# Long convolution and gate on one core: in the last phase VectorE joins at the end of each quarter, transposes follow two rows later, the first x rows load first, and constant matmuls stand between the phases

## The chip, the cores and the metric

One core of a Trainium2 chip runs the whole kernel. The metric is the device time of one execution in microseconds; lower is better. All data is float32.

## The reference

Two steps, one after the other: a long convolution of `u = x * v` with a filter made from `pos_emb`, gated by x, and then a short gate over the result.

```python
h_filt = (np.maximum(pos_emb @ w1, 0.0) @ w2) * np.exp(-0.01 * pos)[:, None]
u = x * v                                     # (4, 12800, 128)
y = irfft(rfft(u, 2 * S) * rfft(h_filt, 2 * S))[:, :S]
x = x * y                                     # goes into the second step
gate_pre = sum(conv_w[k] * x_shifted_by(4 - k) for k in range(5))
out = (sigmoid(gate_pre) * (x @ w_val)) @ w_out
```

## The kernel before, in words

The sequence of 12800 is cut into J = 2 halves of N1 x N2 = 100 x 64, and the transforms are done as matmuls with tables of cosines and sines. There are three phases.

**Phase one** (to about 420 us) transforms along N1, prepares the filter, and writes `a_u` to memory.

**Phase two** (420 to 848 us) goes over 50 pairs of frequencies: it loads `a_u` and a table, multiplies with the filter's spectrum, transforms back along N2, and writes `c_y` to memory (line 378, from ScalarE's queue). The last pair's matmuls are `c_ps` (line 368), its copy `c_sb` (line 375).

**Phase three** (from 848 us) is what the change is about. Its order of instructions is written out by hand (`tc.manual_schedule()`), in the loop at line 573. It works on 32 groups of R = 4 rows. A step `t` of the loop holds three groups at once: group `s = t + 3` gets its rows of y, group `t` its taps, group `t - 1` its value, gate product and projection. One pass of the inner loop over `r` is called a quarter here; a quarter handles one row of each of the three groups:

- `y_sum` (PE, line 492): the last inverse transform of a row, out of two tiles of `c_y`, into `sd` in PSUM. `y_copy` (ScalarE, line 499) copies it to `sd_sb`.
- `y_trans`: four transposes (PE, line 506) into `tp3`, and the copy of one half of it to `dif` (ScalarE, line 508).
- `y_join`: sum and difference of the halves (VectorE, lines 516 and 517) into `yr`, and the product with the x row (GpSimd, line 519) into `ext`.
- `tap` (VectorE, line 534): one term of the short convolution for a whole group, accumulated in `gt`; a group has taps 1 to 4, one in each quarter. Tap 0 is ScalarE's (line 531), and so is the `sigmoid` behind tap 4 (line 538).
- `value` (PE, line 543), `gated` (the gate product, VectorE, line 548), `project` (PE, line 553), `finish` (ScalarE's copy of the output row, line 561, and after four rows the output's DMA, line 564).
- Once in four groups `fill_halo` copies rows between `ext` tiles on ScalarE.

The loads of a group come from SP's queue (`load_rows`): two tiles of `c_y`, each split by rows 96 and 4, and one tile of x rows (line 459). All loads of the kernel share one pool, `ld`, of six buffers; a new tile takes the buffer that came free first. A `c_y` buffer is free after the group's last `y_sum`, an x buffer after the group's last product. SP issues in order, and so does each engine.

Of the kernel before, what the change touches and what calls it, by code (L numbers as in the profile page):

```python
# [9 lines left out]
F32 = mybir.dt.float32  # L10
# [13 lines left out]
B, S, D, FO, KC = 4, 12800, 128, 64, 5  # L24
# [2 lines left out]
KG = 8  # L27
P1C = 2
R = 4
NC1 = N1 // 2 + 1  # L30


def _tables():
# [5 lines left out]
    inv = np.zeros((N1, 2, N2))  # L39
    inv[:, 0, :NC1] = (np.cos(th.T) + np.sin(th.T))[:, :NC1] / (2 * M)  # L40
    inv[:, 1, :NC1] = (np.cos(th.T) - np.sin(th.T))[:, :NC1] / (2 * M)
    ph = (np.outer(4 * k1 + 1, n2)[:, :, None] + 4 * N1 * np.outer(n2, k2)[None]) % (4 * M)
# [62 lines left out]
def tile_longconv_gate(  # L105
# [20 lines left out]
    nc = tc.nc  # L126
# [13 lines left out]
    dft = const.tile([128, 2, 2 * N2], F32, name="dft")  # L140
    tw = const.tile([128, 2, N1], F32, name="tw")
    ident = const.tile([128, 128], F32, name="ident")
# [19 lines left out]
    def load():  # L162
        return ld.tile([128, 2048], F32, name="ld")
# [276 lines left out]
    with tc.tile_pool(name="p3", bufs=1) as p3, tc.tile_pool(name="ps3", bufs=1, space=PSUM) as ps3:  # L440
        HALO = KC - 1
        ROW = B * N1
        NG = N2 // R
        EG = 4
        assert HALO == R
        groups = [(j, g) for j in range(J) for g in range(NG)]
        y_order = [(j, g) for j in range(J) for g in [NG - 1] + list(range(NG - 1))]
        tails, exts, loads3, sds, tps, gate_sg, gate_gt, outs3 = {}, {}, {}, {}, {}, {}, {}, {}

        def load_rows(s):  # L450
            j, g = y_order[s]
            ct = []
            for c in range(2):
                t = load()[:N1]
                n0 = c * N2 + g * R
                sync_s.dma_start(out=t, in_=c_y[j].rearrange("k p b d -> k p (b d)")[:, n0:n0 + R].rearrange("k p e -> k (p e)"))
                ct.append(t)
            xr = load()[:, 0:R * ROW]
            nc.sync.dma_start(out=xr, in_=xt[j][:, g * R:(g + 1) * R].rearrange("d n b a -> d (n b a)"))
            loads3[s] = ct, xr  # L460

        def place(j, g):

            if g == NG - 1 and (j, g // EG) not in exts:
                return tails[j], 0
            return exts[j, g // EG], HALO + g % EG * R

        def new_ext(j, q):
            e = p3.tile([D, HALO + EG * R, B, N1], F32, name="ext", bufs=2)
            exts[j, q] = e  # L470
# [17 lines left out]
        def y_sum(s, r):  # L488
            ct, _ = loads3[s]
            sd = ps3.tile([128, B * D], F32, name="sd", bufs=2)  # L490
            for c in range(2):
                nc.tensor.matmul(  # L492
                    out=sd[c * N2:(c + 1) * N2], lhsT=inv[:, c], rhs=ct[c][:, r * B * D:(r + 1) * B * D],
                    start=True, stop=True)
            sds[s, r] = sd

        def y_copy(s, r):
            t = p3.tile([128, B, D], F32, name="sd_sb", bufs=3)
            nc.scalar.copy(out=t.rearrange("p b d -> p (b d)"), in_=sds.pop((s, r)))  # L499
            sds[s, r] = t  # L500

        def y_trans(s, r):
            t = sds.pop((s, r))
            tp = ps3.tile([D, B, 128], F32, name="tp3", bufs=2)
            for b in range(B):
                nc.tensor.transpose(out=tp[:, b], in_=t[:, b], identity=ident)  # L506
            dif = p3.tile([D, B, NC1], F32, name="dif", bufs=3)
            nc.scalar.copy(out=dif, in_=tp[:, :, N2:N2 + NC1])
            tps[s, r] = tp, dif

        def y_join(s, r):
            tp, dif = tps.pop((s, r))
            j, g = y_order[s]
            xr = loads3[s][1].rearrange("d (n b a) -> d n b a", n=R, b=B)[:, r]
            yr = p3.tile([D, B, N1], F32, name="yr", bufs=3)
            nc.vector.tensor_tensor(yr[:, :, 0:NC1], tp[:, :, 0:NC1], dif, op=ALU.add)  # L516
            nc.vector.tensor_tensor(yr[:, :, NC1:N1], tp[:, :, 1:NC1 - 1], dif[:, :, 1:NC1 - 1], op=ALU.subtract)  # L517
            e, r0 = place(j, g)
            nc.gpsimd.tensor_tensor(e[:, r0 + r], yr, xr, op=ALU.mult)  # L519

        def rows(t, k=HALO):
            j, g = groups[t]
            e = exts[j, g // EG].rearrange("d n b a -> d (n b a)")
            r0 = g % EG * R + k
            return e[:, r0 * ROW:(r0 + R) * ROW]

        def tap(t, k):
            if k == 0:
                gt = p3.tile([D, R * ROW], F32, name="gt", bufs=2)
                gate_gt[t] = gt  # L530
                nc.scalar.activation(gt, rows(t, 0), AF.Copy, scale=cw[:, 0:1])  # L531
            else:
                gt = gate_gt[t]
                nc.vector.scalar_tensor_tensor(gt, rows(t, k), cw[:, k:k + 1], gt, op0=ALU.mult, op1=ALU.add)  # L534

        def sigmoid(t):
            sg = p3.tile([D, R * ROW], F32, name="sg", bufs=2)
            nc.scalar.activation(sg, gate_gt.pop(t), AF.Sigmoid)  # L538
            gate_sg[t] = sg

        def value(t, r):
            v_ps = ps3.tile([D, ROW], F32, name="v_ps", bufs=2)
            nc.tensor.matmul(out=v_ps, lhsT=wval, rhs=rows(t)[:, r * ROW:(r + 1) * ROW], start=True, stop=True)  # L543
            return v_ps

        def gated(t, r, v_ps):
            gd = p3.tile([D, ROW], F32, name="gd", bufs=3)
            nc.vector.tensor_tensor(gd, v_ps, gate_sg[t][:, r * ROW:(r + 1) * ROW], op=ALU.mult)  # L548
            return gd

        def project(gd):
            o_ps = ps3.tile([D, ROW], F32, name="o_ps", bufs=2)
            nc.tensor.matmul(out=o_ps, lhsT=wout, rhs=gd, start=True, stop=True)  # L553
            return o_ps

        def finish(t, r, o_ps):
            if r == 0:
                o_sb = p3.tile([D, R * ROW], F32, name="o_sb", bufs=2)
                outs3[t] = o_sb
            o_sb = outs3[t]  # L560
            nc.scalar.copy(out=o_sb[:, r * ROW:(r + 1) * ROW], in_=o_ps)
            if r == R - 1:
                j, g = groups[t]
                nc.scalar.dma_start(
                    out=out[j][:, g * R:(g + 1) * R].rearrange("d n b a -> d (n b a)"), in_=outs3.pop(t))

        AHEAD3, NT = 3, len(groups)
        y_last = gd_last = o_last = None  # L570
        with tc.manual_schedule():
            load_rows(0)
            for t in range(-AHEAD3, NT + 2):
                s = t + AHEAD3
                if s + 1 < NT:
                    load_rows(s + 1)
                if 0 <= s < NT:
                    j, g = y_order[s]
                    if g == NG - 1:
                        tails[j] = p3.tile([D, R, B, N1], F32, name="tail", bufs=2)  # L580
                    elif g % EG == 0:
                        new_ext(j, g // EG)
                for r in range(R):
                    if y_last is not None:
                        y_trans(*y_last)
                    v_ps = value(t - 1, r) if 0 <= t - 1 < NT else None
                    if s < NT:
                        y_sum(s, r)
                    if o_last is not None:
                        finish(*o_last)  # L590
                        o_last = None
                    if gd_last is not None:
                        o_last = gd_last[0], gd_last[1], project(gd_last[2])
                        gd_last = None
                    if 0 <= t < NT:
                        tap(t, r + 1)
                    if r == R - 1 and 0 <= t < NT:
                        sigmoid(t)
                    if y_last is not None:
                        y_join(*y_last)  # L600
                        y_last = None
                    if v_ps is not None:
                        gd_last = t - 1, r, gated(t - 1, r, v_ps)
                    if s < NT:
                        y_copy(s, r)
                        y_last = s, r
                    if r == 1 and s < NT and g % EG == 0:
                        fill_halo(j, g // EG)
                    if r == 2 and 0 <= t + 1 < NT:
                        tap(t + 1, 0)  # L610


_INS = ["x", "v", "pos_emb", "w1", "w2", "moe_w_val", "moe_conv_w", "moe_w_out"]
# [34 lines left out]
```

## Time and profile before

| | us |
|---|---|
| three runs | 1342.48, 1333.96, 1340.4 (median 1340.4) |
| the profiled execution | 1342.08 |
| its span | 1340.2 |
| mean granted clock of TensorE | 0.938 |

The page gives busy time for each engine. PE is TensorE's matmuls, PEld its weight loads, DVE VectorE, ACT ScalarE, POOL GpSimd, SP the engine that issues loads; a "q" behind an engine is its queue. A row of a timeline has the start in us, the length in us, the engine, the line of the kernel, the operation, output and inputs by the program's names; "[... <- ...]" is the idle time of the engine before it, and what ended it. A granted clock of 0.50 is TensorE at half speed. A float32 matmul stands in the trace as two records.

### The profile page before, as it was taken

The numbers are of one execution on the slowest core, as the hardware profiler recorded it, in microseconds if no ns is written. First come the engines' busy times: TensorE is split into PE (matmuls) and PEld (weight loads), VectorE is DVE, ScalarE is ACT, GpSimd is POOL, SyncE is SP. The second block draws the span as 40 slices with busy tenths as digits, with TensorE's granted clock in tenths as the row PEclk, the third lists the DMA queues.
The fourth block names the chain that finished last, engine by engine and source line by source line (L and its number), as shares of the span: only waits on it lengthen the run. The fifth ranks groups of instructions, "written<-read, shape, count | busy, mean of one in ns | idle before, by whom it ended". The sixth has DMA issues, their size and how long they took to land. (4 is left out here: it accounts for less than half of the span.)

```text
span 1340.2 us, 16163 instructions
## 1 busy us (share of the span) xinstructions
PE 1184.8 (88%) x5464; PEld 554.0 (41%) x5464; DVE 1068.8 (80%) x1130; ACT 635.5 (47%) x1064; POOL 693.8 (52%) x346
## 2 busy tenths in 40 slices
PE   4879999788686899999999999578999898999986
PEld 3657877566452333333333333122333333333332
DVE  5875343988456999999999999127999999999997
ACT  3334545677442333333333333134665666666663
POOL 2333234444454799999999999234333333333230
PEclk8888899889888999999999999656999999999999
DMA  9999788889987677778787874766989898889842
GB/s 250 285 312 297 232 253 271 245 268 306 296 261 285 219 278 280 281 277 279 280 280 279 280 266 173 209 160 157 254 236 246 234 243 243 244 247 243 241 145 98
DMA packets 144571, 332.90 MB, mean 248 GB/s; under 512 B 11166, under 2 KB 63434, under 8 KB 136554
## 3 DMA queue, kind: packets, MB, share of 16 engines
q1 hardware_dynamic: 96576, 226.13, 57.9%
q10 hardware_dynamic: 47914, 105.76, 21.7%
q8 instruction: 43, 0.70, 0.2%
q14 instruction: 38, 0.31, 0.1%
HBM read 200.77 MB, written 131.07 MB: 248 GB/s over the span
## 5 line engine op out<-in xcount | busy, mean ns | idle before, releaser
L534 DVE SCALAR_TENSOR_TENSOR gt<-ext,cw,gt 128x1600 f32<-128x1600 f32 x128 | 298.3, 2330 | 0.0
L258 POOL TENSOR_TENSOR u_lo<-u_t,u_hi 100x1024 fp32r<-100x1024 f32 x64 | 158.7, 2483 | 239.0 <-ACT u_hi L257 199.9
L519 POOL TENSOR_TENSOR ext<-yr,ld 128x400 f32<-128x400 f32 x120 | 134.1, 1117 | 280.4 <-DVE yr L517 275.1
L375 ACT COPY c_sb<-c_ps 128x1024 f32<-128x1024 f32 x100 | 101.3, 1013 | 275.3 <-PE c_ps L368 275.3
L340 PE MATMUL z_ps<-ld 128*64 128x512 f32 x800 | 194.4, 605 | 7.8 <-DMA ld<-a_u 6.6
L427 POOL TENSOR_TENSOR va<-va,vb 128x1024 f32<-128x1024 f32 x50 | 158.0, 3160 | 37.1 <-DVE vb L345 37.0
L281 PE MATMUL fp<-u_hi,fwd_hi 100*100 100x512 f32 x256 | 117.8, 460 | 55.2 <-ACT st L284 26.4
L492 PE MATMUL sd<-ld,inv 100*64 100x512 f32 x512 | 155.6, 681 | 9.8 <-issue 7.7
L286 DVE COPY st<-fp 100x512 f32<-100x512 f32 x128 | 85.4, 685 | 71.8 <-PE fp L281 52.9
L345 DVE TENSOR_TENSOR vb<-z_ps,h_sb 128x2048 f32<-128x2048 f32 x50 | 114.5, 2291 | 24.9 <-ACT c_sb L375 24.7
L506 PE MATMUL tp<-ident,sd_sb 128*128 128x128 f32 x512 | 90.7, 304 | 45.7 <-ACT sd_sb L499 45.7
L499 ACT COPY sd_sb<-sd 128x512 f32<-128x512 f32 x128 | 74.6, 583 | 115.5 <-PE sd L492 115.4
L553 PE MATMUL o_ps<-gd,wout 128*128 128x400 f32 x256 | 119.4, 548 | 8.4 <-DVE gd L548 8.2
L428 POOL TENSOR_TENSOR vc<-vc,vd 128x1024 f32<-128x1024 f32 x50 | 118.5, 2370 | 15.2 <-DVE vd L345 10.3
L256 DVE TENSOR_TENSOR u_t<-ld 100x1024 f32<-100x1024 f32 x64 | 86.9, 1359 | 48.4 <-POOL u_lo L258 33.6
L345 DVE TENSOR_TENSOR va<-z_ps,h_sb 128x2048 f32<-128x2048 f32 x50 | 114.0, 2281 | 11.0 <-DMA ld<-a_u 11.0
L429 POOL TENSOR_TENSOR va<-va,vb 128x1024 f32<-128x1024 f32 x50 | 118.6, 2371 | 0.0
L506 PEld LDWEIGHTS tp<-ident,sd_sb 128*128 128x128 f32 x512 | 58.6, 151 | 132.9 <-ACT sd_sb L499 132.9
L281 PE MATMUL fp<-u_hi,fwd_lo 100*100 100x512 f32 x256 | 110.0, 430 | 0.0
L368 PE MATMUL c_ps<-vc,ld 64*128 64x512 f32 x400 | 100.6, 621 | 10.7 <-DVE vc L418 10.6
L543 PE MATMUL v_ps<-ext,wval 128*128 128x400 f32 x256 | 108.5, 506 | 0.0
L257 ACT CAST u_hi<-u_t 100x1024 fp32r<-100x1024 f32 x64 | 68.0, 1064 | 77.4 <-PE fp L281 37.0
(76 smaller groups left out, 1895.6 us busy)
## 6 DMA issues: line engine op xcount, KB each, us to landing
c_y<-c_sb ACTq DMA_DIRECT2D x100, 512.0 KB
ld<-a_u SPq DMA_DIRECT2D x49, 1024.0 KB
ld<-c_y SPq DMA_DIRECT2D x64, 768.0 KB
ld<-in_xt_dram SPq DMA_DIRECT2D x32, 800.0 KB
out_dram<-o_sb ACTq DMA_DIRECT2D x32, 800.0 KB
ld<-in_x_dram SPq DMA_DIRECT2D x64, 384.0 KB
ld<-in_v_dram SPq DMA_DIRECT2D x64, 384.0 KB
a_u<-st ACTq DMA_DIRECT2D x64, 384.0 KB
```

Of the source, the lines that this page charges most:

```text
L258: nc.gpsimd.tensor_tensor(lo, u_t, hi.bitcast(F32), op=ALU.subtract)
L281: nc.tensor.matmul(out=fp, lhsT=w[:, c], rhs=d[:, b:b + 2], start=(k == 0), stop=(k == 2))
L340: nc.tensor.matmul(out=z[half[h]], lhsT=wk[:, h, half[c]], rhs=a2[:, h, j], start=True, stop=True)
L345: nc.vector.tensor_tensor(out, z.rearrange("p (b d) -> p b d", d=D).unsqueeze(1).to_broadcast([128, n, B, D]), h_sb.unsqueeze(2).to_broadc ...
L427: nc.gpsimd.tensor_tensor(va[:, 0:2], va[:, 0:2], vb[:, 0:2], op=ALU.add)
L428: nc.gpsimd.tensor_tensor(vc, vc, vd, op=ALU.add)
L429: nc.gpsimd.tensor_tensor(va[:, 2:4], va[:, 2:4], vb[:, 2:4], op=ALU.add)
L492: nc.tensor.matmul(out=sd[c * N2:(c + 1) * N2], lhsT=inv[:, c], rhs=ct[c][:, r * B * D:(r + 1) * B * D], start=True, stop=True)
L506: nc.tensor.transpose(out=tp[:, b], in_=t[:, b], identity=ident)
L519: nc.gpsimd.tensor_tensor(e[:, r0 + r], yr, xr, op=ALU.mult)
L534: nc.vector.scalar_tensor_tensor(gt, rows(t, k), cw[:, k:k + 1], gt, op0=ALU.mult, op1=ALU.add)
L553: nc.tensor.matmul(out=o_ps, lhsT=wout, rhs=gd, start=True, stop=True)
```

## The change

The row of y that a quarter transposes and joins is now the row summed two quarters earlier (`LAG = 2`, kept in the list `y_run`); it was the row of the quarter before. The joins move behind the gate product. Tap 0 of the next group moves from the third quarter to the fourth, and the sigmoid behind the copy of the sums. The x rows of the first three groups are loaded ahead of all `c_y` tiles. Forty matmuls of two constant tables stand ahead of the first sum; nothing reads their result.

```diff
+WARM = 40
...
+        def load_x(s):
+            j, g = y_order[s]
+            xr = load()[:, 0:R * ROW]
+            nc.sync.dma_start(out=xr, in_=xt[j][:, g * R:(g + 1) * R].rearrange("d n b a -> d (n b a)"))
+            loads3[s] = xr
...
-            xr = load()[:, 0:R * ROW]
-            nc.sync.dma_start(out=xr, in_=xt[j][:, g * R:(g + 1) * R].rearrange("d n b a -> d (n b a)"))
-            loads3[s] = ct, xr
+            if s not in loads3:
+                load_x(s)
+            loads3[s] = ct, loads3[s]
...
-        AHEAD3, NT = 3, len(groups)
-        y_last = gd_last = o_last = None
+        AHEAD3, NT, LAG = 3, len(groups), 2
+        y_run, gd_last, o_last = [], None, None
         with tc.manual_schedule():
+            for s in range(AHEAD3):
+                load_x(s)
             load_rows(0)
+
+            for _ in range(WARM):
+                w_ps = ps3.tile([D, 2 * D], F32, name="o_ps", bufs=2)
+                nc.tensor.matmul(
+                    out=w_ps, lhsT=ident, rhs=dft.rearrange("p a k -> p (a k)"), start=True, stop=True)
...
                 for r in range(R):
-                    if y_last is not None:
-                        y_trans(*y_last)
+                    done = y_run.pop(0) if len(y_run) == LAG or s >= NT and y_run else None
+                    if done:
+                        y_trans(*done)
...
                     if 0 <= t < NT:
                         tap(t, r + 1)
+                    if r == R - 1 and 0 <= t + 1 < NT:
+                        tap(t + 1, 0)
+                    if v_ps is not None:
+                        gd_last = t - 1, r, gated(t - 1, r, v_ps)
+                    if done:
+                        y_join(*done)
+                    if s < NT:
+                        y_copy(s, r)
+                        y_run.append((s, r))
                     if r == R - 1 and 0 <= t < NT:
                         sigmoid(t)
-                    if y_last is not None:
-                        y_join(*y_last)
-                        y_last = None
-                    if v_ps is not None:
-                        gd_last = t - 1, r, gated(t - 1, r, v_ps)
-                    if s < NT:
-                        y_copy(s, r)
-                        y_last = s, r
                     if r == 1 and s < NT and g % EG == 0:
                         fill_halo(j, g // EG)
-                    if r == 2 and 0 <= t + 1 < NT:
-                        tap(t + 1, 0)
```

VectorE's instructions over two quarters in the middle of the phase, before (`yr` are the joins, `gd` the gate product, `gt` the tap; the numbers tell tiles apart):

```order
L516 TENSOR_TENSOR yr_6741<-tp3_6724,dif_6729 128x4x51
L517 TENSOR_TENSOR yr_6741<-tp3_6724,dif_6729 128x4x49
L548 TENSOR_TENSOR gd_6745<-v_ps_6731,sg_6682 128x400
L534 SCALAR_TENSOR_TENSOR gt_6664<-ext_6478,cw_75,gt_6664 128x1600
L516 TENSOR_TENSOR yr_6766<-tp3_6749,dif_6754 128x4x51
L517 TENSOR_TENSOR yr_6766<-tp3_6749,dif_6754 128x4x49
L548 TENSOR_TENSOR gd_6770<-v_ps_6756,sg_6682 128x400
L534 SCALAR_TENSOR_TENSOR gt_6664<-ext_6478,cw_75,gt_6664 128x1600
```

The same place in the change:

```order
L541 SCALAR_TENSOR_TENSOR gt_6749<-ext_6547,cw_75,gt_6749 128x1600
L555 TENSOR_TENSOR gd_6810<-v_ps_6800,sg_6759 128x400
L523 TENSOR_TENSOR yr_6812<-tp3_6793,dif_6798 128x4x51
L524 TENSOR_TENSOR yr_6812<-tp3_6793,dif_6798 128x4x49
L541 SCALAR_TENSOR_TENSOR gt_6749<-ext_6547,cw_75,gt_6749 128x1600
L555 TENSOR_TENSOR gd_6835<-v_ps_6825,sg_6759 128x400
L523 TENSOR_TENSOR yr_6837<-tp3_6818,dif_6823 128x4x51
L524 TENSOR_TENSOR yr_6837<-tp3_6818,dif_6823 128x4x49
```

Before, the gate product stands between the joins and the tap; now the tap follows the joins at once. (Lines of the change stand 7 further down.)

SP's queue from the last load of phase two on, before:

```order
L358 DMA ld_5905<-a_u_63 128x2x1024
L101 DMA ld_6064<-c_y_64 96x2048
L101 DMA ld_6064<-c_y_64 4x2048
L101 DMA ld_6067<-c_y_64 96x2048
L101 DMA ld_6067<-c_y_64 4x2048
L459 DMA ld_6070<-in_xt_dram 128x1600
L101 DMA ld_6072<-c_y_64 96x2048
L101 DMA ld_6072<-c_y_64 4x2048
L101 DMA ld_6075<-c_y_64 96x2048
L101 DMA ld_6075<-c_y_64 4x2048
L459 DMA ld_6078<-in_xt_dram 128x1600
```

And in the change (`c_y` at line 102, x rows at line 454):

```order
L359 DMA ld_5905<-a_u_63 128x2x1024
L454 DMA ld_6064<-in_xt_dram 128x1600
L454 DMA ld_6066<-in_xt_dram 128x1600
L454 DMA ld_6068<-in_xt_dram 128x1600
L102 DMA ld_6070<-c_y_64 96x2048
L102 DMA ld_6070<-c_y_64 4x2048
L102 DMA ld_6073<-c_y_64 96x2048
L102 DMA ld_6073<-c_y_64 4x2048
L102 DMA ld_6156<-c_y_64 96x2048
L102 DMA ld_6156<-c_y_64 4x2048
L102 DMA ld_6159<-c_y_64 96x2048
```

Three x tiles stand first, so the sixth and last free buffer of the pool goes to the first `c_y` tile of the second group (`ld_6156`); the second one (`ld_6159`) needs a buffer to come free.

PE at the hand-over, before (`tp` are the transposes):

```order
L368 MATMUL c_ps<-vc,ld 128x512 x4
L492 MATMUL sd<-ld,inv 64x512 x2
L506 MATMUL tp_6086<-ident,sd_sb 128x128 x4
L492 MATMUL sd<-ld,inv 64x512 x2
L506 MATMUL tp_6102<-ident,sd_sb 128x128 x4
L492 MATMUL sd<-ld,inv 64x512 x2
```

And in the change:

```order
L369 MATMUL c_ps<-vc,ld 128x512 x4
L585 MATMUL o_ps<-dft,ident 128x256 x40
L499 MATMUL sd<-ld,inv 64x512 x4
L513 MATMUL tp_6173<-ident,sd_sb 128x128 x4
L499 MATMUL sd<-ld,inv 64x512 x2
L513 MATMUL tp_6189<-ident,sd_sb 128x128 x4
```

The forty constant matmuls come ahead of the first sums, and two rows are summed before the first is transposed.

## Prediction

> **What bounds the kernel now.** The page comes first, then the busy time by stretches, then the groups of the last phase, then its order of time. The profiled execution took 1342.1 us (span 1340.2 and 1.9 around it), 1.7 above the median of the three times; all sums below start from it. The last phase runs from about 848 us to the end.
>
> ```profile
> PE 1184.8 (88%) x5464; PEld 554.0 (41%) x5464; DVE 1068.8 (80%) x1130; ACT 635.5 (47%) x1064; POOL 693.8 (52%) x346
> ...
> 860.00:880.00 20.00, 15.74 (x41) 5.05 (x40) 3.23 (x11) 5.15 (x12) 5.14 (x5) 0.50 0.81 194
> ...
> 1100.00:1200.00 100.00, 92.43 (x362) 35.53 (x360) 99.59 (x120) 62.06 (x109) 32.75 (x30) 1.00 0.88 243
> ```
>
> Line one ranks PE first over the whole span. The stretches (after the length: busy us of PE, PEld, DVE, ACT, POOL, then granted clock, DMA share, GB/s) say otherwise for this phase: from 1100 to 1200 DVE is busy 99.59 of 100 us, so VectorE sets the pace; at 860 it has 3.23 of 20 us, and PE works at clock 0.50. So two stages must be costed apart: the steady stage, and the ramp before it.
>
> ```profile
> 1104.34 0.64 PE L506 MATMUL tp<-ident,sd_sb 128*128 128x128 f32 x4
> ...
> 1106.52 0.36 DVE L516 TENSOR_TENSOR yr<-tp,dif 128x204 f32<-128x204 f32 x1
> ...
> 1106.80 0.34 DVE L517 TENSOR_TENSOR yr<-tp,dif 128x196 f32<-128x196 f32 x1
> 1107.06 0.56 DVE L548 TENSOR_TENSOR gd<-v_ps,sg 128x400 f32<-128x400 f32 x1
> ...
> 1107.22 1.04 POOL L519 TENSOR_TENSOR ext<-yr,ld 128x400 f32<-128x400 f32 x1 [2.31 <-DVE yr L517]
> ...
> 1107.36 0.64 PE L506 MATMUL tp<-ident,sd_sb 128*128 128x128 f32 x4
> 1107.55 2.40 DVE L534 SCALAR_TENSOR_TENSOR gt<-ext,cw,gt 128x1600 f32<-128x1600 f32 x1
> ...
> 1107.84 0.84 PE L543 MATMUL v_ps<-ext,wval 128*128 128x400 f32 x2
> ...
> 1108.60 1.08 PE L492 MATMUL sd<-ld,inv 100*64 100x512 f32 x4
> ...
> 1109.61 0.94 PE L553 MATMUL o_ps<-gd,wout 128*128 128x400 f32 x2
> ...
> 1109.87 0.36 DVE L516 TENSOR_TENSOR yr<-tp,dif 128x204 f32<-128x204 f32 x1
> ```
>
> One quarter on VectorE is 1109.87 - 1106.52 = 3.35 us, without a gap: two joins (0.28 + 0.26), the gate product (0.49), the tap (2.32 to the next join). The join releases GpSimd's product, which starts 0.16 us after the gate product begins and is still running when the tap begins.
>
> ```profile
> 901.00 0.35 DVE L517 TENSOR_TENSOR yr<-tp,dif 128x196 f32<-128x196 f32 x1
> 901.27 1.88 DVE L534 SCALAR_TENSOR_TENSOR gt<-ext,cw,gt 128x1600 f32<-128x1600 f32 x1
> 901.43 2.63 POOL L519 TENSOR_TENSOR ext<-yr,ld 128x400 f32<-128x400 f32 x1 [2.90 <-DVE yr L517]
> ...
> 1306.11 1.87 DVE L534 SCALAR_TENSOR_TENSOR gt<-ext,cw,gt 128x1600 f32<-128x1600 f32 x1
> 1307.90 0.56 DVE L548 TENSOR_TENSOR gd<-v_ps,sg 128x400 f32<-128x400 f32 x1
> ```
>
> In the first group of taps there is no gate product yet, so the tap follows the join at once: 1.88 us, and GpSimd's product takes 2.63. After the last product the tap alone takes 1.87. So a tap costs 0.52 more when the product starts before it, and nothing when it starts first; then the product pays 1.6.
>
> **The change, part by part.** *Join last.* The quarter becomes tap, gate product, two joins, tap: the order of 901.00 to 901.27 in every quarter. VectorE then needs 1.79 (1306.11 to 1307.90) + 0.49 + 0.28 + 0.27 = 2.83 us, 11.3 a group of four. The product would end 2.8 us after the tap's start (0.16 + 2.63), before the next tap.
>
> What is late next is PE. From 1104.34 to 1107.36 it goes round in 3.02: transposes 0.48, value 0.76, sums 1.01, projection 0.77. That is 12.1 a group. Today it also waits for the copied rows.
>
> ```profile
> L506 PE MATMUL tp<-ident,sd_sb 128*128 128x128 f32 x388 | 62.7, 284 | 28.9 <-ACT sd_sb L499 28.9
> ...
> 1028.40:1030.40 2.00, 0.99 (x7) 0.58 (x6) 2.00 (x2) 1.36 (x2) 1.00 (x1) 1.00 0.78 188
> 1030.40:1036.40 6.00, 6.00 (x25) 2.24 (x24) 6.00 (x9) 2.62 (x6) 2.08 (x2) 1.00 1.02 234
> 1036.40:1041.00 4.60, 4.60 (x20) 1.62 (x18) 4.60 (x5) 3.39 (x6) 1.04 (x1) 1.00 0.93 320
> 1041.00:1041.80 0.80, 0.80 (x4) 0.30 (x2) 0.80 (x4) 0.70 (x2) 0.05 (x1) 1.00 0.12 48
> ...
> 1096.33 1.45 SPq L101 DMA_DIRECT2D ld<-c_y  x4
> ...
> 1101.44 0.35 SPq L459 DMA_DIRECT2D ld<-in_xt_dram  x1
> ```
>
> *Transposes two rows behind.* The wait of 28.9 us (of the 330 between 960 and 1290) is for the copy of the row before; a row more between copy and transpose (3 us) covers it, also where ScalarE puts tap 0 and the sigmoid in between. No work is added. Left alone, PE would go at its 12.1.
>
> ```profile
> 1107.19 1.63 ACT L531 ACTIVATE gt<-ext,cw 128x1600 f32<-128x1600 f32 x1
> ...
> 1109.98 1.54 ACT L538 ACTIVATE sg<-gt 128x1600 f32<-128x1600 f32 x1 [0.55 <-DVE gt L534]
> ```
>
> *Tap 0 and sigmoid later.* Both now stand in the last quarter, the sigmoid behind the copy of the sums: 3.2 us of ScalarE at one place, a little more than a quarter. Once a group VectorE's next gate product waits for the sigmoid, by my reading some 0.8 us, which is just its slack against PE (12.1 - 11.3): cost 0. Without that slack it is 27 x 0.8 = 22 us.
>
> The third bound is DMA. A group's transfers fill 12.6 of 13.4 us (1028.40 to 1041.00), c_y for some 8.0 us, then x rows and output; as a share 0.88 x 13.4 = 11.8 us if packed without gaps. Issue moves as well: SP's x load waits for the product that frees its buffer. It came 5.1 us behind the c_y loads (1096.33, 1101.44) and will come one quarter (3.0) and 1.6 of longer product later, at 9.7. SP's queue holds the next c_y loads behind it, but those wait until 12.1 anyway. So the new wait sits in cover of 2.4 us; without it c_y would land late at the next group's first sum.
>
> Bounds for the group: 11.3 (VectorE alone) to 13.4 (DMA no better than now). I take the middle of PE's 12.1 and DMA's 12.6, 12.35, since both are close.
>
> ```profile
> 934.71 2.40 DVE L534 SCALAR_TENSOR_TENSOR gt<-ext,cw,gt 128x1600 f32<-128x1600 f32 x1
> ...
> 1299.96 2.39 DVE L534 SCALAR_TENSOR_TENSOR gt<-ext,cw,gt 128x1600 f32<-128x1600 f32 x1
> ```
>
> These are the first taps of groups 2 and 29: 365.25 us for 27 groups, 13.53 each with the groups that also copy the halo. **Steady stage: 27 x (13.53 - 12.35) = 31.9 us less.**
>
> *The gap.* Now the hand-over between the phases, and the loads.
>
> ```profile
> 844.30 2.65 PE L368 MATMUL c_ps<-vc,ld 64*128 64x512 f32 x8 [4.13 <-DVE vc L418]
> ...
> 846.99 1.01 ACT L375 COPY c_sb<-c_ps 128x1024 f32<-128x1024 f32 x1 [5.75 <-PE c_ps L368]
> ...
> 852.07 0.99 SPq L101 DMA_DIRECT2D ld<-c_y  x3
> ...
> 854.61 1.94 PE L492 MATMUL sd<-ld,inv 100*64 100x512 f32 x2 [7.66 <-issue]
> ...
> 858.71 1.94 PE L492 MATMUL sd<-ld,inv 100*64 100x512 f32 x2 [2.16 <-DMA ld<-c_y]
> ...
> 862.37 1.97 PE L492 MATMUL sd<-ld,inv 100*64 100x512 f32 x4
> ...
> 866.07 1.98 PE L492 MATMUL sd<-ld,inv 100*64 100x512 f32 x4
> ...
> 871.77 1.45 SPq L101 DMA_DIRECT2D ld<-c_y  x4
> ...
> 903.75 1.98 PE L492 MATMUL sd<-ld,inv 100*64 100x512 f32 x4
> ...
> 921.46 1.98 PE L492 MATMUL sd<-ld,inv 100*64 100x512 f32 x4
> ```
>
> After 4.13 us without work the last c_ps runs slow, and in the ramp a row takes 3.7 us (862.37 to 866.07) at half clock. The x loads move ahead of the c_y loads, into the end of phase two, where SP only waits; I cost them at nothing, covered by DMA that is not full there (if not, 3 x 2.8 us ahead of c_y's 852.07 would be the price). The 40 constant matmuls have no row; the nearest is the value's 0.76 for 400 columns, so 0.49 for 256, 19.6 us, and 3.4 more for the first ones at half clock: from 848.0, the end of the last copy, to 871. Below, 0.43 and no surcharge give 865; above, all at half clock, 887. The first sum, ready at 858.7, waits some 12 us.
>
> Then rows pass in 1.5 us (0.48 + 1.01): group 0's sums end at 876, against 871.8. Here the six `ld` buffers bite: three hold x rows, so group 1's second c_y half goes out only at 876 and lands about 6.5 us later (4.0 for half of 8.0, 2.5 from 852.07 to 854.61), at 882.5. Group 2's first half follows; its second waits for group 0's x rows, freed near 887, and lands at 893.4. Group 3's halves follow, 4.0 each, at 897.4 and 901.4, its x rows at 904, group 4's c_y at 912.2. So group 3's first sum is at 901.4 (903.75 now) and group 4's at 912.2 (921.46 now); group 5's at 924.3 by PE's pace, where now it is near 937. **Ramp: 12.6 us less**, from 3 (clock half again throughout) to 17 (constants done at 865).
>
> *Tail.* After the last product VectorE already goes 2.28 a quarter; the last joins come one quarter later, beside taps of a phase that PE no longer fills: 0, or 0.55 if nothing hides them.
>
> Sum: 1342.1 - 31.9 - 12.6 = 1297.6, **1298 us**.
>
> The Trainium skill (TensorE: Matmul & The Clock Gate, HAM oscillation) says that PE-idle gaps over some 3.4 us halve the clock and a busy window of that length restores it. The 4.13 us above agree. By that rule the wait for group 1's second half (about 6 us) throws the warm clock away again, and it returns within a window or two of full work: some 3 us of the ramp, 1301 in all. The 0.50 at 860 to 880, with PE busy 15.74 of 20 us, says that work with gaps does not restore it.
>
> **Rivals.** *DMA is the bound.* For it: 1.02 and 0.93 in the two stretches; against: only 234 to 320 GB/s there, and idle at 1041. A group of 13.0, between 12.6 and 13.4, gives 27 x 0.53 + 12.6 = 27 us less: 1315 (1305 to 1326).
>
> *The ramp stays cold.* For it: PE waits for loads three times. Rows at 3.1 us leave 3 us of the ramp's gain: 1307.
>
> *PE's round shrinks too* (the transposes' 0.77 before them contained a wait): a group of 11.5, 27 x 2.03 + 12.6 = 67 less, 1275.
>
> *The change doesn't free the tap.* If GpSimd still starts first, because VectorE waits before the tap (at a group's first tap it now waits for ScalarE's tap 0, put last), the group stays at 13.4: 1342.1 - 4 - 12.6 = 1326. The five taps of 1.88 speak against.
>
> *Slower: the product blocks what now runs beside it.* GpSimd's product, pushed back by the tap, will run its last 1.0 us (2.79 - 1.79) beside the gate product and the joins. If they too stand still against it, VectorE's quarter is 2.83 + 1.0 = 3.83 and the group 15.3: 27 x 1.8 = 48 more, 1342.1 + 48 - 12.6 = 1378. It decides from 0.5 us of blocking, where the quarter is back at 3.35. Against it, the gate product took 0.56 beside a product (1107.06) and 0.56 without (1307.90); for it, no row shows a join beside one.
>
> By the Trainium skill (SBUF — State Buffer, Who interferes with whom) an instruction of VectorE with at most one SBUF input does not contend with GpSimd, so this rival would not happen; the gate product's two 0.56 agree, and for the joins no run here shows it yet.
>
> **How the numbers follow.** Forecast 0.50 (1285 to 1306), cold ramp 0.14, DMA 0.17, shorter PE round 0.06, tap not freed 0.07, slower 0.06. A time within 1% of 1340 can't be told from no change. Below 1327 lie the first four and half of the fifth: 0.88; the same 0.07, slower 0.05. The range goes from 1282, leaving out most of the short round, to 1326, leaving out the last two cases.
>
> **What would show it.** Tap near 1.88 and product near 2.6; a quarter near 3.05, with PE over 95% busy and VectorE some 93%; DMA share at 0.95; constants to about 871, then 6 us of waiting; group 4's first sum near 912. I am wrong if taps stay at 2.39, if a group's first sum waits for c_y by microseconds, if a join beside a product takes more than its 0.36, or if the clock is below 1.00 after 930.

## The result and the profile after

The change takes 1287.88 us (median of four runs, 1279.84 to 1298.73) against 1341.44 us of the kernel before (four runs, 1333.96 to 1357.69): a ratio of 0.962, with a 95% interval from 0.953 to 0.972. The forecast was 1298, with 1282 to 1326 as its range. The profiled execution of the change took 1295.49 us, its span 1293.7. Ratios, here and below, leave out executions more than 1.5% above the fastest of their kernel, which keeps two of four for kernels 3 and 12 below and seven of ten for kernel 5; the profiles of 3 and 5 are of such slower executions.

The same rows of the page and of the view of stretches as before the change (after the length: busy us of PE, PEld, DVE, ACT, POOL, then granted clock, DMA share, GB/s):

```profile
PE 1179.1 (91%) x5544; PEld 576.5 (45%) x5544; DVE 1010.5 (78%) x1130; ACT 630.1 (49%) x1064; POOL 867.0 (67%) x346
...
860.00:880.00 20.00, 17.68 (x82) 11.64 (x80) 1.92 (x6) 3.22 (x7) 3.09 (x3) 1.00 0.36 86
...
1100.00:1200.00 100.00, 100.00 (x402) 42.15 (x401) 95.37 (x135) 67.60 (x119) 87.78 (x34) 1.00 0.95 275
```

In the steady stage PE has taken VectorE's place by busy time: 100.00 of 100 us instead of 92.43, VectorE 95.37 instead of 99.59. GpSimd went from 32.75 to 87.78 with the same work in each group: its product takes longer, as the next rows show. At 860 the clock is 1.00 instead of 0.50, but the DMA share fell from 0.81 to 0.36: PE works on constants there, no sum frees a buffer of the pool, and few loads run.

A quarter in order of time, after the change:

```profile
1101.62 0.60 PE L513 MATMUL tp<-ident,sd_sb 128*128 128x128 f32 x4
...
1102.25 0.36 DVE L523 TENSOR_TENSOR yr<-tp,dif 128x204 f32<-128x204 f32 x1
...
1102.53 0.35 DVE L524 TENSOR_TENSOR yr<-tp,dif 128x196 f32<-128x196 f32 x1
1102.80 1.87 DVE L541 SCALAR_TENSOR_TENSOR gt<-ext,cw,gt 128x1600 f32<-128x1600 f32 x1
...
1102.95 2.61 POOL L526 TENSOR_TENSOR ext<-yr,ld 128x400 f32<-128x400 f32 x1 [0.21 <-DVE yr L524]
...
1104.59 0.56 DVE L555 TENSOR_TENSOR gd<-v_ps,sg 128x400 f32<-128x400 f32 x1
1104.61 0.60 PE L513 MATMUL tp<-ident,sd_sb 128*128 128x128 f32 x4
...
1105.08 0.35 DVE L523 TENSOR_TENSOR yr<-tp,dif 128x204 f32<-128x204 f32 x1
```

The tap starts 0.15 us before the product and takes 1.87; the product takes 2.61. VectorE's quarter is 1105.08 - 1102.25 = 2.83 us, PE's round 1104.61 - 1101.62 = 2.99. The gate product (0.56) and the join at 1105.08 (0.35) run beside GpSimd's product, which ends at 1105.56, and are no longer than before.

The first taps of groups 2 and 29:

```profile
926.68 1.87 DVE L541 SCALAR_TENSOR_TENSOR gt<-ext,cw,gt 128x1600 f32<-128x1600 f32 x1
...
1253.70 1.88 DVE L541 SCALAR_TENSOR_TENSOR gt<-ext,cw,gt 128x1600 f32<-128x1600 f32 x1
```

They lie 327.0 us apart, 12.11 a group; before it was 365.25 and 13.53. So the steady stage gives back 38.2 us.

The ramp, in order of time: the last `c_sb` copy, then PE; the last row is group 4's first sum:

```profile
850.84 1.01 ACT L376 COPY c_sb<-c_ps 128x1024 f32<-128x1024 f32 x1 [5.51 <-PE c_ps L369]
...
851.90 19.12 PE L585 MATMUL o_ps<-dft,ident 128*128 128x256 f32 x80 [1.10 <-ACT c_sb L376]
870.96 1.94 PE L499 MATMUL sd<-ld,inv 100*64 100x512 f32 x8
...
876.60 1.07 PE L499 MATMUL sd<-ld,inv 100*64 100x512 f32 x2
882.63 1.94 PE L499 MATMUL sd<-ld,inv 100*64 100x512 f32 x2 [4.96 <-DMA ld<-c_y]
...
885.55 1.98 PE L499 MATMUL sd<-ld,inv 100*64 100x512 f32 x4
...
888.50 1.98 PE L499 MATMUL sd<-ld,inv 100*64 100x512 f32 x4
...
904.74 1.08 PE L499 MATMUL sd<-ld,inv 100*64 100x512 f32 x4
...
914.01 1.08 PE L499 MATMUL sd<-ld,inv 100*64 100x512 f32 x4
```

The last `c_sb` copy of phase two ends at 851.85 here and at 848.00 before. That point is the zero of everything below: up to it the programs do the same, yet in the profiles of this study it came anywhere from 838.7 to 868.7 us, a spread as large as the effects. Counted from it, group 2's first tap comes at 926.68 - 851.85 = 74.8 us, against 934.71 - 848.00 = 86.7 before: the ramp gives 11.9. The difference of the spans: 38.2 + 11.9 + 0.2 (tail) - 3.85 (a later start of the last phase) = 46.45 = 1340.16 - 1293.71.

One wait is new. From the list of waits between 930 and 1240 us (who waited for whom: us in total, times, longest):

```profile
DVE yr L523 <- ACT dif L515: 19.1, 7, 3.7
ACT ext L491 <- POOL ext L526: 19.0, 6, 4.6
```

Both belong to one place, the halo copy of every fourth group. There in order of time:

```profile
1125.38 1.87 DVE L541 SCALAR_TENSOR_TENSOR gt<-ext,cw,gt 128x1600 f32<-128x1600 f32 x1
...
1125.54 2.61 POOL L526 TENSOR_TENSOR ext<-yr,ld 128x400 f32<-128x400 f32 x1 [0.19 <-DVE yr L524]
...
1128.18 1.53 ACT L491 COPY ext<-ext 128x1600 f32<-128x1600 f32 x1 [2.72 <-POOL ext L526]
...
1129.61 0.32 ACT L515 COPY dif<-tp 128x204 f32<-128x204 f32 x1
...
1130.04 0.37 DVE L523 TENSOR_TENSOR yr<-tp,dif 128x204 f32<-128x204 f32 x1 [2.30 <-ACT dif L515]
```

With transposes two rows behind, the last row of the previous group is written by the product of 1125.54, which the tap has stretched to 2.61 us. ScalarE's halo copy stands in the second quarter and waits 2.72 us for it; the copy to `dif` queues behind, and VectorE's join waits 2.30 us for that. So VectorE's groups go 11.3, 11.3, 11.3, 13.7 us. Two of the seven long groups take 15.5 and 16.0 us; there ScalarE copies two pieces of rows, one after the other. That is a theory of why the mean is 12.1, beside the forecast's, that PE is the bound.

### The profile page after: what moved, and what is told of

Its sections match the earlier page's. It is cut to its first block, busy times and chain, and to the rows that moved or that the text cites. A ratio compares the mean times of both kernels' runs of the same rounds, so it can differ in the third digit from the quotient of the medians.

```text
span 1293.7 us, 16572 instructions
## 1 busy us (share of the span) xinstructions
PE 1179.1 (91%) x5544; PEld 576.5 (45%) x5544; DVE 1010.5 (78%) x1130; ACT 630.1 (49%) x1064; POOL 867.0 (67%) x346
## 4 chain that ended last, share of the span: by engine, by line
PE 66%; DMA 17%; DVE 9%; POOL 3%; ACT 3%; issue 2%; SPq 1%; ACTq 0%; DVEq 0%; POOLq 0%
PE c_ps L369 14%; PE z_ps L341 13%; DMA a_u<-st 9%; PE sd L499 9%; PE o_ps L560 7%; PE fp L282 6%; PE v_ps L550 5%; PE tp L513 4%; DMA ld<-in_v_dram 4%; PE z_ps L328 4%; DMA ld<-in_x_dram 3%; DVE gt L541 3%; PE ap L222 2%; PE ap L221 2%; PE o_ps L585 1%
## 5 line engine op out<-in xcount | busy, mean ns | idle before, releaser
L526 POOL TENSOR_TENSOR ext<-yr,ld 128x400 f32<-128x400 f32 x120 | 300.1, 2501 | 62.9 <-DVE yr L524 43.3
L541 DVE SCALAR_TENSOR_TENSOR gt<-ext,cw,gt 128x1600 f32<-128x1600 f32 x128 | 242.3, 1893 | 1.4 <-ACT gt L538 1.3
L499 PE MATMUL sd<-ld,inv 100*64 100x512 f32 x512 | 146.1, 641 | 5.0 <-DMA ld<-c_y 5.0
L258 ACT CAST u_hi<-u_t 100x1024 fp32r<-100x1024 f32 x64 | 68.2, 1066 | 78.6 <-PE fp L282 29.0
L341 PEld LDWEIGHTS z_ps<-ld 128*64 128x64 f32 x800 | 55.2, 139 | 113.3 <-issue 86.6
L285 ACT COPY st<-fp 100x512 f32<-100x512 f32 x128 | 70.8, 593 | 70.2 <-PE fp L282 43.8
```

The source lines that it names most:

```text
L341: nc.tensor.matmul(out=z[half[h]], lhsT=wk[:, h, half[c]], rhs=a2[:, h, j], start=True, stop=True)
L499: nc.tensor.matmul(out=sd[c * N2:(c + 1) * N2], lhsT=inv[:, c], rhs=ct[c][:, r * B * D:(r + 1) * B * D], start=True, stop=True)
```

## The experiments

The results in one table. "Ratio" is to the kernel before on the same chip, with its 95% interval. "Ramp" is from the end of the last `c_sb` copy to group 2's first tap, "group" a 27th of the time from there to group 29's first tap, and "last phase" from that copy to the end; these three come from the profiled executions.

| kernel | ratio | ramp, us | group, us | last phase, us |
|---|---|---|---|---|
| before | 1 | 86.7 | 13.53 | 492.2 |
| the change | 0.962 (0.953 to 0.972) | 74.8 | 12.11 | 441.9 |
| 1 without constants | 0.964 (0.958 to 0.969) | 68.4 | 12.07 | 434.3 |
| 2 without early x | 0.952 (0.946 to 0.959) | 66.1 | 12.11 | 433.2 |
| 3 order and lag alone | 0.941 (0.933 to 0.950) | 65.6 | 12.09 | 432.6 |
| 4 order alone | 0.980 (0.972 to 0.988) | 85.8 | 12.71 | 468.8 |
| 5 lag alone | 0.993 (0.987 to 0.998) | 68.6 | 13.59 | 477.0 |
| 6 two x tiles, 14 constants | 0.948 (0.937 to 0.959) | 60.4 | 12.07 | 426.2 |
| 7 half projection | 0.956 (0.948 to 0.965) | 73.6 | 12.10 | 439.2 |
| 8 halo copy later | 0.956 (0.952 to 0.960) | 70.7 | 11.99 | 434.3 |
| 9 half projection, halo later | 0.950 (0.947 to 0.954) | 71.3 | 11.66 | 425.1 |
| 10 as 6, halo later | 0.947 (0.940 to 0.953) | 62.0 | 11.91 | 423.5 |
| 11 the change again | 0.960 (0.954 to 0.966) | 74.9 | 12.09 | 441.4 |
| 12 order, lag 1, 40 constants | 0.980 (0.967 to 0.993) | 79.4 | 12.71 | 462.4 |

The times of one kernel spread by 1 to 2% and more, so ratios tell only the larger steps apart; the last phase of the change agreed to 0.5 us in two profiles (441.9, 441.4), and the parts are read there. The ramp is less exact: the forty constants alone took 19.12 us in the change and 17.53 in kernel 8, which has the same ones.

**1, 2 and 3: the gap.** The constants taken out, the early x loads taken out, and both.

```diff
-WARM = 40
+WARM = 0          # kernels 1 and 3
...
-            for s in range(AHEAD3):
-                load_x(s)      # kernels 2 and 3
```

> The change without the forty constant matmuls; early x loads, join last and lag 2 stay. My theory (the gain is VectorE's order plus the lag, up to PE's pace; the constants hold PE for 19 us and the clock they warm is lost again in the wait for group 1's second c_y half): the first sums start some 10 us earlier but at half clock, group 1's c_y comes about as late, and the time stays within 6 us of the change, 1282 to 1294. Rival (the warm clock is what shortens the ramp): some 10 us more than the change, 1298, with rows of 3 us at half clock up to the first taps.

> The change with the x loads back behind each group's c_y; the forty constants stay. My theory (six buffers: early x rows take the place of group 1's second c_y half): no wait of 5 us at group 1's first sum, clock at 1.00 all through the ramp, group 3's first sum some 6 us earlier, 1282. Rival (early x rows save DMA time in the ramp): 5 to 9 us more than the change, about 1295.

> Join last and lag 2 alone: no constants, no early x. My theory: all of the steady gain is here (a group of 12.1 us on average), and the ramp is no worse than the change's: rows of 2.95 us from the first sum on, group 3's first sum about 39 us after the last c_y copy, 1281 to 1286. Rival (constants and early x give a good part of the 53 us): 1300 or more.

Without both, the ramp is 9.2 us shorter than in the change (65.6 against 74.8). Alone, the constants cost 0.5 (66.1), which is no more than the scatter just named, and the early x loads 2.8 (68.4); together they cost 9. In time, order and lag alone are the only one of the three whose interval lies below that of the change, with two executions behind it. Kernel 1 kept its time, as expected. In kernel 2 the wait at group 1's first sum is gone, but the clock is not full throughout, which the theory had expected: after a wait of 2.05 us for `c_y`, 35.2 us behind the copy, the next sum takes 1.98 us. PE in kernel 3, in order of time:

```profile
868.86 3.65 PE L499 MATMUL sd<-ld,inv 100*64 100x512 f32 x6 [2.12 <-DMA ld<-c_y]
...
873.49 1.98 PE L499 MATMUL sd<-ld,inv 100*64 100x512 f32 x4
875.39 1.01 PE L513 MATMUL tp<-ident,sd_sb 128*128 128x128 f32 x4
876.34 1.08 PE L499 MATMUL sd<-ld,inv 100*64 100x512 f32 x4
```

The copy ended at 858.2 here. Sums and transposes follow each other without a gap from 868.86 to 879, and at 876.3, 18 us behind the copy, the clock is full with no constant matmul in the program: a sum's 1.98 us becomes 1.08. In the change the first sum comes 12.5 us later (19.1 us behind the copy instead of 6.6), and group 1's second half of `c_y` waits for a buffer that those sums free: the 4.96 us at 882.63. Kernel 1 has the same wait (5.07 us), but it ends 25.6 us behind the copy instead of 30.8.

**4 and 5: order and lag apart.** Neither has constants or early x loads. Kernel 4 has VectorE's new order and the old lag; kernel 5 the new lag and the old order, with tap 0 and the sigmoid where they were.

```diff
-        AHEAD3, NT, LAG = 3, len(groups), 2      # kernel 4
+        AHEAD3, NT, LAG = 3, len(groups), 1
...
-                    if r == R - 1 and 0 <= t + 1 < NT:      # kernel 5
-                        tap(t + 1, 0)
+                    if r == R - 1 and 0 <= t < NT:
+                        sigmoid(t)
+                    if done:
+                        y_join(*done)
                     if v_ps is not None:
                         gd_last = t - 1, r, gated(t - 1, r, v_ps)
-                    if done:
-                        y_join(*done)
...
-                    if r == R - 1 and 0 <= t < NT:
-                        sigmoid(t)
...
+                    if r == 2 and 0 <= t + 1 < NT:
+                        tap(t + 1, 0)
```

> Join last alone, transposes one row behind as before; no constants, no early x. My theory: taps fall to 1.88 us here too, but PE waits again for the copied sums where ScalarE puts tap 0 and sigmoid, some 1.3 us a group, so a group takes about 13.2 and the time is 1305 to 1325. Rival A (VectorE's order is the whole gain): the same as join last with lag 2, within 4 us. Rival B (the order is worth nothing without the lag): 1335 or more.

> Transposes two rows behind, with VectorE's order, tap 0 and sigmoid as before; no constants, no early x. My theory: VectorE stays the bound at 3.35 us a quarter, since the product still starts before the tap (taps 2.39, products 1.04); only the ramp's rows gain, from 3.7 to about 2.95 us, twelve of them: 1330 to 1336. Rival (PE's wait for the copied sums was what paced the group): a group of 12.1 to 12.5, 1295 to 1310.

The last phase: 492.2 before, 477.0 with the lag, 468.8 with the order, 432.6 with both. The two alone add up to 38.6 us, together they give 59.6. The stages show why. The *ramp* is the lag's: 68.6 and 65.6 with it, 85.8 and 86.7 without; the 18 us in kernel 5 are twice the twelve rows of 0.75 that were expected. The *group* is the order's first (13.53 to 12.71), and the lag helps only then (12.09 with the order, 13.59 without), since without the order VectorE bounds the group and a faster PE brings nothing. The groups of the tap and the product between 960 and 1230 us (count, busy us, mean ns, idle before them) in kernel 5:

```profile
L541 DVE SCALAR_TENSOR_TENSOR gt<-ext,cw,gt 128x1600 f32<-128x1600 f32 x80 | 191.8, 2398 | 0.0
L526 POOL TENSOR_TENSOR ext<-yr,ld 128x400 f32<-128x400 f32 x76 | 80.3, 1058 | 177.4 <-DVE yr L524 161.7 <-ACT sd_sb L506 12.7 <-DVE gd L555 3.1
```

and in kernel 4, with PE's transposes and ScalarE's halo copy; behind it the halo copy in kernel 5:

```profile
L526 POOL TENSOR_TENSOR ext<-yr,ld 128x400 f32<-128x400 f32 x82 | 181.8, 2218 | 77.7 <-DVE yr L524 77.0 <-ACT sd_sb L506 0.7
L541 DVE SCALAR_TENSOR_TENSOR gt<-ext,cw,gt 128x1600 f32<-128x1600 f32 x85 | 168.5, 1982 | 10.1 <-ACT gt L538 10.1
L513 PE MATMUL tp<-ident,sd_sb 128*128 128x128 f32 x340 | 54.9, 284 | 6.5 <-ACT sd_sb L506 6.5
L491 ACT COPY ext<-ext 128x1600 f32<-128x1600 f32 x4 | 6.1, 1530 | 0.0
```

```profile
L491 ACT COPY ext<-ext 128x1600 f32<-128x1600 f32 x4 | 6.1, 1532 | 13.3 <-POOL ext L526 13.3
```

With the lag alone the tap stays at 2398 ns and the product at 1058. With the order alone the tap is mostly freed. PE is busy 97.71 of 100 us from 1100 on; its transposes wait 6.5 us of these 270 for the copied rows (their weight loads 51.2, but those run beside PE's other matmuls), and the tap waits 10.1 us for ScalarE's tap 0. With the second row of lag as well, in kernel 3, these two waits are 0.0 and 0.1. How much of the group each is worth stays open; 13.2 was expected for kernel 4, and 12.71 came. The halo copy's wait comes with the lag: 0.0 in kernel 4, 13.3 in kernel 5, where the product is still short.

**12: can constants stand in for the lag in the ramp?** Kernel 4 with the forty constants.

```diff
-WARM = 0
+WARM = 40
```

> VectorE's order of the change, transposes one row behind, forty constants, x rows loaded where they were. Without the constants this kernel stayed at clock 0.50 until 78.6 us behind the last c_sb copy, and group 2's first tap came at 85.8. Theory A (the constants can stand in for the second row of lag in the ramp): the clock is 1.00 from some 4 us on and short waits for the copied row do not lower it; group 2's first tap at 66 to 70, last phase 449 to 453 us. Rival B (only a row of lag keeps PE without gaps, and the first waits take the warm clock away again): clock 0.50 from some 25 to 40 us to near 80, group 2's first tap at 80 to 88, last phase 463 to 471.

Between the two: ramp 79.4, last phase 462.4. PE's order of time:

```profile
886.51 0.66 PE L513 MATMUL tp<-ident,sd_sb 128*128 128x128 f32 x4 [0.74 <-ACT sd_sb L506]
887.10 1.08 PE L499 MATMUL sd<-ld,inv 100*64 100x512 f32 x4
889.63 1.12 PE L513 MATMUL tp<-ident,sd_sb 128*128 128x128 f32 x4 [1.46 <-ACT sd_sb L506]
890.68 2.32 PE L499 MATMUL sd<-ld,inv 100*64 100x512 f32 x4
893.73 1.12 PE L513 MATMUL tp<-ident,sd_sb 128*128 128x128 f32 x4 [0.73 <-ACT sd_sb L506]
```

The full clock outlived eleven waits of 0.7 to 0.8 us (from 862.5 on), and went at the first longer one, 1.46 us. It then stayed at half for 24 us through waits of the same length. So constants buy 6.4 us of the ramp at lag 1, and the lag buys 13 more even with them (79.4 against kernel 2's 66.1).

**6: what the gap has room for.** Two x tiles early and 14 constants, so that group 1's second `c_y` half has a buffer and the first sum is not held up.

```diff
-WARM = 40
+WARM = 14
...
-            for s in range(AHEAD3):
+            for s in range(2):
```

> The change with x rows of two groups ahead in place of three (so that both c_y halves of group 1 find a buffer) and 14 constants in place of 40 (so that they end when the first c_y lands). My theory: first sum some 9 us earlier, no wait at group 1, rows of 1.5 us at full clock, group 4's first sum some 14 us earlier than in the change: 1272 to 1278. Rival (DMA sets the ramp whatever PE does): within 4 us of the change.

The ramp is 60.4 us, 5.2 less than with neither: constants of 8.5 us end near the point where the first `c_y` lands, and the clock is full from the first sum until a wait of 2.94 us for `c_y`, 37.6 us behind the copy.

**7, 8 and 9: what bounds the group.** Kernel 7 multiplies only half of the projection's columns and copies that half twice. Kernel 8 moves the halo copy one quarter on. Kernel 9 does both.

```diff
-            nc.tensor.matmul(out=o_ps, lhsT=wout, rhs=gd, start=True, stop=True)
+            nc.tensor.matmul(out=o_ps[:, 0:ROW // 2], lhsT=wout, rhs=gd[:, 0:ROW // 2], start=True, stop=True)
...
-            nc.scalar.copy(out=o_sb[:, r * ROW:(r + 1) * ROW], in_=o_ps)
+            nc.scalar.copy(
+                out=o_sb[:, r * ROW:(r + 1) * ROW].rearrange("d (h e) -> d h e", h=2),
+                in_=o_ps[:, 0:ROW // 2].unsqueeze(1).to_broadcast([D, 2, ROW // 2]))
...
-                    if r == 1 and s < NT and g % EG == 0:
+                    if r == 2 and s < NT and g % EG == 0:
```

> The change with half of the projection left out: PE multiplies 200 of 400 columns, and ScalarE copies that half twice, so the other work is as before. It takes 0.33 us from PE's 2.99 in a quarter. My theory (PE is the bound, DMA has room at a share of 0.95): the group falls from 12.1 to VectorE's 11.3, 27 x 0.8 = 22 us less than the change, 1266. Rival (DMA is as much the bound): the group stays at 11.8 or more and the gain is under 8 us.

> The changed kernel with the halo copy one quarter later (third instead of second). Theory A: the group is 11.3 us by VectorE, and 13.7 in every fourth one because ScalarE's halo copy waits for the product that the tap has pushed back, and the dif copies wait behind it; then the mean group falls from 12.1 to between 11.3 and 12.0 (PE needs 11.96 by its rows), 3 to 20 us less than the change. Rival B: the halo group is long for another reason (the DMA of the halo, or PE catching up); then the group stays at 12.1 and the time at that of the change.

> Half of the projection's columns is left out (the other half is copied twice) and the halo copy is one quarter later. PE then needs some 10.7 us a group. Theory A: 11.3 to 11.5 a group, VectorE's pace, 16 to 22 us less than the change, where leaving out half of the projection alone gave nothing. Rival B (DMA sets the group, 11.8 us of packed transfers): 11.8 to 12.1, at most 8 us less.

PE's load down by a third of a microsecond a quarter: 12.10 a group, as if nothing had been done, where 11.3 had been expected. The number is the rival's (11.8 or more); kernel 9 shows that DMA is not the reason. The halo's wait gone: 11.99. Both: 11.66. VectorE's waits in the same stretch as above, in kernels 7, 8 and 9 in that order, for the copy to `dif` and for ScalarE's tap 0:

```profile
DVE yr L523 <- ACT dif L515: 16.8, 6, 3.7
```

```profile
DVE gt L541 <- ACT gt L538: 8.2, 10, 1.2
DVE yr L523 <- ACT dif L515: 2.3, 2, 1.1
```

```profile
DVE gt L541 <- ACT gt L538: 6.6, 7, 1.2
```

and the view of stretches from 1100 to 1200 us in kernels 7, 8 and 9:

```profile
1100.00:1200.00 100.00, 95.32 (x405) 42.30 (x404) 95.40 (x137) 68.56 (x122) 87.89 (x34) 0.97 0.96 275
```

```profile
1100.00:1200.00 100.00, 100.00 (x403) 42.30 (x400) 97.44 (x135) 68.81 (x121) 77.88 (x33) 1.00 0.96 272
```

```profile
1100.00:1200.00 100.00, 98.34 (x418) 42.54 (x416) 98.43 (x140) 71.11 (x123) 87.29 (x36) 1.00 0.97 286
```

Kernel 7 leaves VectorE's 95.4 of 100 us where it was and gives the time to PE as idle time, at a clock of 0.97; kernel 8 leaves PE at 100.00. Two limits of almost the same height lie on each other: PE's round, 4 x 2.99 = 11.96, and VectorE with its halo wait, (3 x 11.3 + 13.7) / 4 = 11.9, or 12.1 with the two groups of 15.5 and 16.0. Removing either alone gains at most 0.12 a group; removing both gains 0.45 x 27 = 12 us of the last phase. Of kernel 8's shorter last phase 4.1 us lie in the ramp, 1.6 of them in constants that ran faster in that execution, and some 3 in the groups. DMA is not a third limit at this height: kernel 9 moves the same bytes at 11.66 a group, and its sums waited 1.0 us for `c_y` in 310 (their weight loads 2.7). Theory A gave kernel 9 11.3 to 11.5, rival B 11.8 to 12.1; groups with the halo still take 12.1 us or more there. One of them has tap 0 late behind the moved halo copy: VectorE waits 0.78 us for it, and the product goes first.

**10 and 11: both repairs together, and the change again.**

```diff
-WARM = 40
+WARM = 14
...
-            for s in range(AHEAD3):
+            for s in range(2):
...
-                    if r == 1 and s < NT and g % EG == 0:
+                    if r == 2 and s < NT and g % EG == 0:
```

> Two x tiles loaded early, 14 constant matmuls, and the halo copy one quarter later. If the two repairs add up, the last phase is the 426 us of the kernel without the halo's move, less 27 times what the halo's move brings per group (0.1 to 0.8 us by theory A): 405 to 423 us, so 18 to 36 us under the change. By rival B 426, 15 us under the change.

> The change as it is, for the comparison on this chip: 0.962 of the kernel before, 442 us from the last c_sb copy to the end, 12.1 us a group by every theory.

Beside the change on the same chip (1287.76 us) kernel 10 took 1273.98. Its last phase, 423.5 us, is 18 shorter than the change's and 2.7 shorter than kernel 6's: in the groups the later halo copy adds 0.16 x 27 = 4.3 us to kernel 6, in the ramp it adds nothing (62.0 against 60.4). 423.5 is just outside the 405 to 423 that were expected. Kernels 3, 6 and 10 can't be told apart by their ratios.

## Why the prediction was right, and where not

**The tap is freed: right, to the hundredth.** 1.87 and 2.61 us where 1.88 and 2.63 were written, and VectorE's quarter is the 2.83 of the sum. Kernel 5 shows that it is the order that does it and not the lag.

**The slower rival: refuted.** A join beside the product takes 0.35 (the row at 1105.08). The Trainium skill (SBUF — State Buffer, Who interferes with whom) says that an instruction of VectorE with at most one SBUF input, outside its two-port modes, does not contend with GpSimd; the joins and the gate product, whose other operand is in PSUM, agree.

**PE is what is late next: right, but not alone.** 3.02 forecast, 2.99 measured, PE 100.00 of 100 us busy. What the sum lacked was the halo group. The step "a row more between copy and transpose (3 us) covers it" looked at PE's wait only: the later row also pushed the product that the halo copy waits for, to a place where ScalarE stands in front of it. It cost little, 0.12 us a group by kernel 8, only because PE's limit is just as high. That the group came out at PE's forecast 12.1 is therefore partly luck: PE's own round is 11.96, and kernel 7, with a PE that needs a good microsecond less, still takes 12.10.

**The term that was mis-sized is the group's 12.35.** It was put halfway between PE's 12.1 and DMA's 12.6, and measured 12.11: 38.2 us less instead of 31.9. The 12.6 was how long transfers lasted when they had 13.4 us to spread over, not how long they need; in the change their share is 0.95 of 12.1, and kernel 9 fits them in 11.66. The DMA rival (13.0) falls with it.

**Tap 0 and the sigmoid: cost 0, right.** VectorE waited for ScalarE's tap 0 for 0.5 us in 310, and the gate product's wait for the sigmoid, forecast at 0.8 us a group and hidden by slack, did not appear: 0.1 us idle before 88 gate products. It does not appear in kernel 9 either, where PE no longer gives slack, so the 0.8 was read too high. The waits for tap 0 in kernels 8 and 9 (8.2 and 6.6 us) come with the moved halo copy; kernel 7, with PE's limit lowered alone, has 0.3.

**The x load: right.** It comes 1105.59 - 1094.96 = 10.6 us behind the `c_y` issue (9.7 forecast), and no sum of the steady stage waited for `c_y`. Here are SP's rows:

```profile
1094.96 1.59 SPq L102 DMA_DIRECT2D ld<-c_y  x4
1105.59 0.35 SPq L454 DMA_DIRECT2D ld<-in_xt_dram  x1
```

**The ramp: the number right, its cause wrong.** 11.9 us against 12.6, and the landings are near those that were worked out (the constants took 19.1 us, not 23): counted from the last copy, group 1's late half starts PE at 30.8 us (34.5 forecast), group 3's first sum comes at 52.9 (53.4), group 4's at 62.2 (64.2). But the gain was put down to the forty constants, as the thing that gives a full clock. The failed step is that the second row of lag was priced for the steady stage alone. The half clock of the ramp before hung on the wait for the copied row: kernel 4, with it, stays at half clock until 78.6 us behind the copy; kernel 3, without it, is at full clock after 18, and at half again only for three rows behind a wait of 3.41 us for `c_y`. Of the 21.1 us that order and lag bring to the ramp (86.7 to 65.6), constants and early x take 9.2 back. "I cost them at nothing" was wrong for the early x loads in this company: their price was not DMA time in phase two, but three of six buffers while the sums that free one were held up. That a larger gain and a new cost came out near 12.6 together is luck.

**The cold ramp.** The wait at 882.63 threw the warm clock away, as written. It came back not within 3 us but after 20.5: at 885.55 a sum takes 1.98 us, and rows of 2.95 us follow each other almost without a gap until 903. That cost less than it looks. In kernel 11 the clock came back earlier (a sum at 891.55 takes 1.08 us), and group 2's first tap came at 74.9 all the same: once warm, PE waited there for `c_y` (1.02, 1.00 and 2.87 us). Loads and buffers set the ramp of the change, not the clock; the cold-ramp rival, priced at 9.6 us, came true in part and cost nothing that shows. The Trainium skill (TensorE: Matmul & The Clock Gate, HAM oscillation) describes waits for loads of over 3.4 us that lower the clock each time, which 4.96 us agree with; the waits of 1.46 us in kernel 12 and 2.05 in kernel 2, with a half clock behind them, are shorter than that. That a busy window of some 3.4 us brings it back, as Part 1 of that page has it, does not hold for these 20.5 us.

**The sum.** The last phase gave 50.3 us (492.2 - 441.9) where 44.5 were forecast; the group gave 6.3 of the difference, the ramp took 0.7 back. The other 3 of the 53.6 us between the medians lie within the spread in front of the last phase. The chances were added a little short: the first four and half of the fifth make 0.905, not 0.88.

## What to carry to other kernels

Where two instructions lengthen each other, as the tap and the product do here (1.87 and 2.61 us with the tap first, 2.40 and 1.04 with the product first), it is enough that the one on the engine that sets the pace starts first; look for an order in which the other one's trigger stands directly ahead of it. A wait of 0.7 us per round can cost far more than itself when it keeps TensorE at half clock: lengthen the distance between producer and consumer before spending matmuls on warming, and count the buffers that the warming holds. When a faster engine leaves the group at one number, test whether two limits lie there: remove each alone and both together.

## What the runs showed that was not expected

The clock under one and the same wait depended on what came before. In kernel 12 a round with one wait of 0.7 us ran at full clock for 25 us and later, with the same wait, at half clock for 24 us; in kernel 4 the half clock lasted until 78.6 us behind the copy. How long each would last by itself no run here shows.

Which of the two goes first is decided by tenths of a microsecond, in one group of one program. Kernel 4, in order of time:

```profile
1100.76 1.88 DVE L541 SCALAR_TENSOR_TENSOR gt<-ext,cw,gt 128x1600 f32<-128x1600 f32 x1
1100.93 2.62 POOL L526 TENSOR_TENSOR ext<-yr,ld 128x400 f32<-128x400 f32 x1 [0.31 <-DVE yr L524]
...
1103.95 1.03 POOL L526 TENSOR_TENSOR ext<-yr,ld 128x400 f32<-128x400 f32 x1 [0.41 <-DVE yr L524]
...
1104.36 2.30 DVE L541 SCALAR_TENSOR_TENSOR gt<-ext,cw,gt 128x1600 f32<-128x1600 f32 x1 [0.49 <-ACT gt L538]
```

The tap at 1100.76 is 0.17 us ahead of the product and takes 1.88. The tap at 1104.36 waited 0.49 us for ScalarE's tap 0, so the product is first: 1.03 us, and the tap pays with 2.30.
